# Clearing memory on VectorE, a last store in two halves, and a new order for all engines in a gated recurrence with a squared-ReLU network

## The chip, the cores and the metric

The kernel runs on one core of one Trainium2 chip. The metric is the device time of the whole program in microseconds, the median of several runs. The engines are TensorE (PE in the profile: matmuls, and PEld for its weight loads), VectorE (DVE), ScalarE (ACT), GpSimd (POOL) and SyncE (SP, which here only issues transfers). Each engine works through its own instructions strictly in program order. They run side by side and wait for one another by semaphores. Transfers (DMA) are issued from SyncE, ScalarE and GpSimd.

## The reference

A recurrence with complex gates over 768 positions, for 4 sequences and 8 heads of 48, and behind it a feed-forward network. The network's weights come in double precision, as pairs of 32-bit words, and are decoded on the chip.

```python
# q, k, v, a_re, a_im: (4, 8, 768, 48); w_in: (384, 2048); w_out: (2048, 384)
mag = sqrt(a_re**2 + a_im**2);  scale = minimum(mag, 0.999) / (mag + 1e-6)
a_re, a_im = a_re * scale, a_im * scale
for t in range(768):
    S_re, S_im = (ar[t] * S_re - ai[t] * S_im) + k[t] v[t]^T,  ar[t] * S_im + ai[t] * S_re
    y[t] = q[t] @ S_re
x = y as (4 * 768 tokens, 8 * 48)
h = maximum(x @ w_in, 0);  out = (h * h) @ w_out
```

## The kernel before

The 3072 tokens are worked in 12 groups of two chunks (`a` and `b`) of 128 tokens. Every engine's instructions follow one string of tokens, `FRONT`, in which each token calls one step. The number behind the letter is the group (or the weight block), and the number behind the point is the step.

```python
    work = {
        "o": lambda gi, k: operands_of[gi][k](),     # gates and operands of a group, 23 steps
        "a": lambda gi, k: chunks_of[gi][0][k](),    # scores, state and values of its chunk a
        "b": lambda gi, k: chunks_of[gi][1][k](),    # the same of chunk b
        "g": fill_gaps,                              # a transfer inside the token tile x
        "F": first_product, "H": squared_relu,       # TensorE; ScalarE
        "T": block_of_second, "E": end_of_second,    # second product of groups 0 and 1
        "X": sums_of_halves, "Y": second_sum, "Q": fourth_sum,   # VectorE: second product in
        "Z": half_product, "R": outputs,             # seven products from group 2 on
        "s": store, "f": fetch, "j": lambda i: fetch(i, True),   # weights, SyncE / GpSimd queue
        "D": weights,                                # decode a block of weights, VectorE
        "W": ...,                                    # watch its size, ScalarE
        "t": sum_weights, "l": load_parts, "i": ..., "v": load_values, "M": turn_mask, "K": ranges,
    }
    # ... cut
    with tc.manual_schedule(engines=by_hand):
        follow(FRONT)
```

The steps of `o` and of `a`/`b` that matter below, by their numbers:

```python
        return [squares, real_parts, imaginary_parts, sum_of_squares, first_inverse,     # 0 to 4
                inverse_squared, queries, inverse, limit, lessened, grown_factor, gates, negated,  # 5 to 12
                grow, keys, lambda: steps_in_blocks((1, 2, 3, 4)),                       # 13 to 15
                lambda: steps_in_blocks((5, 6, 7)), totals, carries, carried, products, last_heads,  # 16 to 21
                grown_squared]                                                           # 22
        # VectorE has 3, 7, 11, 13, 15, 16, 17, 19 and 20; 21 is a set of transfers
        # ... cut
        return [scores, lambda: keys_turned(RE), lambda: keys_copied(RE), lambda: keys_turned(IM),  # 0 to 3
                lambda: keys_copied(IM), masked, sums_of_values, tokens, added, new_state]          # 4 to 9
        # TensorE has 0, 1, 3, 6 and 8; ScalarE 2, 4 and 7; VectorE 5 and 9
```

The decode of a block of weights, five VectorE instructions (the last is a `tensor_tensor` in the helper `tt`, L480):

```python
        nc.vector.tensor_scalar(out=head, in0=high, scalar1=3, scalar2=0x3FFFFFF8,      # L585
                                op0=ALU.logical_shift_left, op1=ALU.bitwise_and)
        nc.vector.scalar_tensor_tensor(out=head, in0=high, scalar=-2 ** 30, in1=head,   # L587
                                       op0=ALU.bitwise_and, op1=ALU.bitwise_or)
        nc.vector.tensor_scalar(out=rest, in0=head, scalar1=-2 ** 23, scalar2=None,     # L589
                                op0=ALU.bitwise_and)
        rest = rest.bitcast(F32)
        nc.vector.scalar_tensor_tensor(out=rest, in0=low.bitcast(U32), scalar=2.0 ** -52, in1=rest,
                                       op0=ALU.mult, op1=ALU.mult)                      # L592
        tt(dst, head.bitcast(F32), rest, ALU.add)
```

The clearing of padding and of the first states, and the store:

```python
    def turn_mask(step):
        # ... cut
        if step == 2:
            for t in ([t[:, :, :, :, C:W] for t in qk_of] + last + [t[:, DM:] for t in vt]
                      + kt + prod + states[0] + states[1]):
                nc.gpsimd.memset(t, 0.0)                                                # L544
            return
    # ... cut
    def store(i, b):
        nc.sync.dma_start(out=in_turn(out, groups[i][b]), in_=out_of[i, b])             # L1002
```

The last output has two parts of 192 columns: the right one is finished by `R11.4`, the left one by `R11.6`, a ScalarE copy and the last piece of work of the program.

Of the kernel before, what the change touches and what calls it, by code (L numbers as in the profile page):

```python
# [425 lines left out]
def quotient_path(ctx, tc, feat, vtok, w_in, w_out, w1, w2, out, n_seq, count):  # L426
# [108 lines left out]
    def turn_mask(step):  # L535
        if step == 0:

            nc.scalar.activation(out=sums[:, 0:1], in_=tiny, func=AF.Abs_reciprocal_sqrt)
            return
        if step == 2:  # L540

            for t in ([t[:, :, :, :, C:W] for t in qk_of] + last + [t[:, DM:] for t in vt]
                      + kt + prod + states[0] + states[1]):
                nc.gpsimd.memset(t, 0.0)  # L544
            return
        nc.scalar.copy(out=mask.rearrange("p (j n) -> p n j", j=L),
                       in_=plain.rearrange("p (n j) -> p n j", j=L))
        turned = pm.tile([C, C], F32, tag="m", name="turned")
        nc.tensor.transpose(turned, mask, ident)
        nc.scalar.copy(out=mask.rearrange("p (j n) -> p n j", j=L),  # L550
                       in_=turned.rearrange("p (n j) -> p n j", j=L))
# [447 lines left out]
        nc.scalar.copy(out=out_of[i, b], in_=o_of[i, b])  # L999

    def store(i, b):
        nc.sync.dma_start(out=in_turn(out, groups[i][b]), in_=out_of[i, b])  # L1002

# [36 lines left out]
    def outputs(i, r):  # L1042
# [27 lines left out]


    FRONT = (
        "l0.0 M0 f0 j0 l0.1 i0.1 f1 j1 M2 f2 j2 v0 o0.0 o0.3 o0.1 o0.4 o0.5 o0.7 o0.2 M1 o0.8 "
        "D0 o0.9 o0.10 o0.6 o0.11 W0 W1 D1 o0.22 f3 v1 j3 o0.12 W2 o0.13 o0.15 o0.14 f4 j4 W3 "
        "l1 i1 o0.16 W4 o0.17 D2 o0.18 o1.6 o0.19 f5 j5 o0.20 o1.0 W5 a0.1 o1.3 o0.21 o1.1 D3 "
        "a0.2 a0.3 o1.4 o1.5 a0.4 a0.8 o1.2 o1.7 f6 j6 b0.0 a0.9 o1.8 b0.1 b0.2 b0.5 o1.9 b0.6 "
        "D4 b0.3 b0.7 a0.0 b0.4 o1.10 W6 b0.8 o1.11 f7 j7 a0.5 o1.12 o1.22 a0.6 b0.9 o1.13 W7 "
        "v2 a0.7 o1.15 o1.14 g0 l2 i2 o1.16 F0.0 o1.17 F0.1 H0.0 D5 o1.18 F0.2 H0.1 o2.6 o1.19 "
        "f8 F0.3 H0.2 F0.4 H0.3 o1.20 o2.0 F0.5 H0.4 W8 a1.1 o2.3 o1.21 D6 a1.2 a1.3 o2.1 a1.4 "
        "a1.8 o2.4 o2.2 F0.6 D7 f9 H0.5 o2.5 a1.0 H0.6 a1.9 F0.7 a1.5 W9 f10 o2.7 a1.6 b1.1 "  # L1080
        "a1.7 D8 b1.0 o2.10 o2.8 H0.7 b1.5 o2.9 f11 b1.6 D9 b1.2 b1.3 b1.7 T0.0 b1.4 g1 W10 "
        "o2.11 T0.1 W11 f12 F1.0 D10 o2.12 o2.22 F1.1 H1.0 D11 T0.2 H1.1 f13 W12 F1.2 o2.15 "
        "T0.3 H1.2 o2.13 F1.3 W13 f14 o2.16 o2.14 b1.8 F1.4 v3 H1.3 l3 b1.9 F1.5 H1.4 D12 W14 "
        "F1.6 D13 T0.4 f15 T1.0 H1.5 D14 F1.7 H1.6 T1.1 o3.6 o2.17 T1.2 H1.7 D15 W15 T1.3 o2.18 "
        "o2.19 T0.5 T0.6 t0 o3.0 T0.7 t1 T1.4 E0.0 t2 E0.1 s0.0 s0.1 o3.3 T1.5 o2.20 o3.4 o3.5 "
        "T1.6 o3.7 o3.1 o2.21 T1.7 o3.2 o3.10 a2.1 t3 E1.0 E1.1 s1.0 a2.2 s1.1 a2.0 o3.8 o3.9 "
        "a2.3 a2.5 a2.4 a2.6 o3.11 a2.8 a2.7 b2.0 a2.9 o3.12 o3.22 b2.1 b2.5 b2.2 b2.6 o3.13 "
        "b2.3 b2.7 b2.4 g2 b2.8 o3.15 o3.14 v4 l4 F2.0 b2.9 F2.4 H2.0 o3.16 F2.1 H2.4 o3.17 "
        "F2.5 H2.1 X2.0 o3.18 Y2.0 o3.19 F2.2 H2.5 F2.6 H2.2 o4.6 o3.20 F2.3 H2.6 o4.0 F2.7 "
        "X2.1 o3.21 H2.3 Y2.1 o4.3 o4.1 X2.2 a3.1 Z2.0 o4.2 Y2.2 H2.7 a3.0 X2.3 o4.4 R2.0 Y2.3 "  # L1090
        "a3.2 o4.5 a3.3 a3.5 Z2.1 a3.4 o4.7 a3.8 Q2.2 o4.10 Q2.1 R2.1 o4.8 a3.6 a3.9 Z2.2 a3.7 "
        "o4.9 Q2.3 Q2.0 b3.0 o4.11 R2.2 b3.1 Z2.3 b3.2 b3.5 o4.12 o4.22 o4.15 b3.6 R2.3 Z2.4 "
        "b3.7 g3 o4.13 Z2.5 R2.4 o4.14 o4.16 Z2.6 l5 b3.3 R2.6 R2.5 F3.0 b3.4 o4.17 b3.8 H3.0 "
        "F3.4 b3.9 o4.18 s2.0 o4.19 F3.1 H3.4 v5 s2.1 F3.5 H3.1 X3.0 o4.20 F3.2 H3.5 o5.6 F3.6 "
        "H3.2 X3.1 o4.21 o5.1 Y3.1 Y3.0 a4.1 F3.3 H3.6 X3.2 o5.2 Y3.2 F3.7 H3.3 a4.2 o5.0 a4.0 "
        "o5.3 H3.7 X3.3 o5.4 a4.3 Z3.0 a4.4 a4.5 o5.5 Y3.3 o5.7 a4.8 R3.0 a4.6 a4.9 o5.10 Z3.1 "
        "a4.7 o5.8 o5.9 Z3.2 R3.1 Q3.2 Q3.1 Q3.0 Q3.3 o5.11 b4.0 R3.2 b4.1 b4.5 o5.12 Z3.3 "
        "o5.22 o5.15 b4.2 b4.6 R3.3 b4.3 b4.7 Z3.4 b4.4 g4 o5.13 b4.8 R3.4 o5.14 Z3.5 v6 b4.9 "
        "l6 o5.16 F4.0 Z3.6 H4.0 R3.5 o5.17 F4.4 R3.6 o5.18 s3.0 o5.19 s3.1 F4.1 H4.4 F4.5 H4.1 "
        "X4.0 o5.20 F4.2 H4.5 o6.6 F4.6 H4.2 X4.1 o5.21 Y4.1 o6.1 Y4.0 F4.3 H4.6 X4.2 o6.2 F4.7 "  # L1100
        "Y4.2 H4.3 o6.0 a5.0 o6.3 H4.7 X4.3 o6.4 Z4.0 o6.5 a5.5 Y4.3 o6.7 a5.6 R4.0 Z4.1 a5.7 "
        "o6.10 o6.8 Z4.2 R4.1 Q4.2 o6.9 Q4.1 Q4.0 Q4.3 o6.11 b5.0 R4.2 Z4.3 b5.5 o6.12 o6.22 "
        "o6.15 b5.6 R4.3 Z4.4 b5.7 v7 g5 o6.13 Z4.5 R4.4 o6.14 o6.16 Z4.6 l7 F5.0 R4.5 R4.6 "
        "o6.17 F5.4 H5.0 o6.18 o6.19 F5.1 H5.4 s4.0 s4.1 F5.5 H5.1 X5.0 o6.20 F5.2 H5.5 o7.6 "
        "F5.6 X5.1 o6.21 H5.2 Y5.1 Y5.0 o7.1 a6.1 F5.3 H5.6 X5.2 o7.2 F5.7 Y5.2 H5.3 a6.2 a6.0 "
        "H5.7 X5.3 o7.0 a6.3 Z5.0 a6.5 a6.4 Y5.3 o7.3 a6.8 R5.0 o7.4 a6.6 a6.9 o7.5 Z5.1 a6.7 "
        "o7.7 o7.10 Z5.2 R5.1 Q5.2 o7.8 Q5.1 Q5.0 Q5.3 o7.9 b6.0 o7.11 R5.2 b6.1 Z5.3 b6.2 b6.5 "
        "o7.12 b6.3 Z5.4 b6.4 o7.15 R5.3 o7.22 b6.6 b6.8 b6.7 g6 R5.4 Z5.5 o7.13 v8 Z5.6 b6.9 "
        "o7.14 R5.5 o7.16 s5.0 F6.0 R5.6 l8 o7.17 F6.4 H6.0 F6.1 H6.4 X6.0 o7.18 Y6.0 s5.1 F6.5 "
        "o7.19 H6.1 F6.2 H6.5 X6.1 F6.6 H6.2 Y6.1 o7.20 o8.6 F6.3 H6.6 o8.0 X6.2 o7.21 Y6.2 "  # L1110
        "a7.1 o8.3 H6.3 F6.7 o8.1 Z6.0 H6.7 X6.3 o8.2 Y6.3 a7.0 R6.0 o8.4 a7.2 o8.5 a7.3 a7.5 "
        "Z6.1 a7.4 o8.7 Z6.2 R6.1 o8.10 Q6.2 Q6.1 o8.8 Q6.0 Q6.3 o8.9 a7.8 a7.6 a7.9 R6.2 Z6.3 "
        "a7.7 o8.11 b7.0 R6.3 o8.12 b7.1 b7.5 o8.22 Z6.4 o8.15 b7.2 b7.6 b7.3 b7.7 Z6.5 b7.4 g7 "
        "R6.4 o8.13 b7.8 R6.5 o8.14 Z6.6 v9 b7.9 s6.0 l9 o8.16 F7.0 R6.6 F7.4 H7.0 o8.17 F7.1 "
        "H7.4 X7.0 o8.18 s6.1 Y7.0 F7.5 o8.19 H7.1 F7.2 H7.5 X7.1 F7.6 H7.2 Y7.1 o8.20 o9.6 "
        "F7.3 H7.6 o9.0 X7.2 o8.21 Y7.2 a8.1 o9.3 H7.3 F7.7 o9.1 Z7.0 H7.7 X7.3 o9.2 Y7.3 a8.0 "
        "R7.0 o9.4 a8.2 o9.5 a8.3 a8.5 Z7.1 a8.4 o9.7 Z7.2 R7.1 o9.10 Q7.2 Q7.1 o9.8 Q7.0 Q7.3 "
        "o9.9 a8.8 a8.6 a8.9 R7.2 Z7.3 a8.7 o9.11 b8.0 R7.3 o9.12 b8.1 b8.5 o9.22 Z7.4 o9.15 "
        "b8.2 b8.6 b8.3 b8.7 Z7.5 b8.4 g8 R7.4 o9.13 b8.8 R7.5 o9.14 Z7.6 v10 b8.9 s7.0 l10 "
        "o9.16 F8.0 R7.6 F8.4 H8.0 o9.17 F8.1 H8.4 X8.0 o9.18 s7.1 Y8.0 F8.5 o9.19 H8.1 F8.2 "  # L1120
        "H8.5 X8.1 F8.6 H8.2 Y8.1 o9.20 o10.6 F8.3 H8.6 o10.0 X8.2 o9.21 Y8.2 a9.1 o10.3 H8.3 "
        "F8.7 o10.1 Z8.0 H8.7 X8.3 o10.2 Y8.3 a9.0 R8.0 o10.4 a9.2 o10.5 a9.3 a9.5 Z8.1 a9.4 "
        "o10.7 Z8.2 R8.1 o10.10 Q8.2 Q8.1 o10.8 Q8.0 Q8.3 o10.9 a9.8 a9.6 a9.9 R8.2 Z8.3 a9.7 "
        "o10.11 b9.0 R8.3 o10.12 b9.1 b9.5 o10.22 Z8.4 o10.15 b9.2 b9.6 b9.3 b9.7 Z8.5 b9.4 g9 "
        "R8.4 o10.13 b9.8 R8.5 o10.14 Z8.6 v11 b9.9 s8.0 l11 o10.16 F9.0 R8.6 F9.4 H9.0 o10.17 "
        "F9.1 H9.4 X9.0 o10.18 s8.1 Y9.0 F9.5 o10.19 H9.1 F9.2 H9.5 X9.1 F9.6 H9.2 Y9.1 o10.20 "
        "o11.6 F9.3 H9.6 o11.0 X9.2 o10.21 Y9.2 a10.1 o11.3 H9.3 F9.7 o11.1 Z9.0 H9.7 X9.3 "
        "o11.2 Y9.3 a10.0 R9.0 o11.4 a10.2 o11.5 a10.3 a10.5 Z9.1 a10.4 o11.7 Z9.2 R9.1 o11.10 "
        "Q9.2 Q9.1 o11.8 Q9.0 Q9.3 o11.9 a10.8 a10.6 a10.9 R9.2 Z9.3 a10.7 o11.11 b10.0 R9.3 "
# [126 lines left out]
```

## Time and profile before

| what | value |
|---|---|
| time, median of 3 | 706.3 us (705.64 to 706.55) |
| span of the profiled execution | 704.7 us |
| TensorE busy | 623.7 us, 89% |
| VectorE busy | 528.5 us, 75% |
| ScalarE busy | 386.6 us, 55% |
| GpSimd busy | 46.3 us, 7% |
| first-product matmuls (L961) | 1152, 257.6 us busy |
| second product in seven parts (L1038) | 1120, 195.0 us busy |
| DMA | 47.75 MB, mean 68 GB/s, 198 GB/s in the first of 40 slices |

In the profile's line by line views the columns are the start in microseconds, the duration, the engine, the source line, the operation, what is written and read (`out<-in`) with the shapes, and in brackets the idle time of the engine just before, with what ended it. In the view of waits they are the engine and its tile, what it waited for, the sum in microseconds, how many waits, and the longest. In the row of 40 slices each digit is a share in tenths. A busy share is an average over the program, so the stages are looked at apart. The mean granted TensorE clock is 0.996.

### The profile page before, as it was taken

Reading aid. Unit: us, or ns where it says so; the run is one execution under the profiler, and the core shown is the slowest. Engines: PE = TensorE matmul, PEld = TensorE weight load, DVE = VectorE, ACT = ScalarE, POOL = GpSimd, SP = SyncE. Lnnn points to the kernel's source line nnn. Section 1 sums busy time; section 2 is a strip of 40 time slices with the busy share of each in tenths; the row PEclk is TensorE's granted clock in tenths of the full one; section 3 lists DMA queues with packets and bytes.
Section 4 is the critical chain, followed back from the end, with each engine's and each line's share of the span. In section 5 each row is a group of like instructions: output and inputs, shape, how many; then the busy total and the mean of one; then the engine's idle time right before and its main releaser. Section 6 shows DMA issues by size and latency. Waiting matters only on the chain.

```text
span 704.7 us, 12547 instructions
## 1 busy us (share of the span) xinstructions
PE 623.7 (89%) x4955; PEld 548.1 (78%) x4955; DVE 528.5 (75%) x916; ACT 386.6 (55%) x684; POOL 46.3 (7%) x106
## 2 busy tenths in 40 slices
PE   0007689999889999999999999999999999999995
PEld 0005577776578898998999989989989989989895
DVE  4998999999699786896785885995985976872130
ACT  6647487754648547537457557366376475340330
POOL 8322200000000000000000000000000000000000
PEclk9999999999999999999999999999999999999999
DMA  8776434461333063062061051151240340110101
GB/s 198 163 132 113 105 74 143 152 108 38 68 75 62 7 93 72 2 124 40 29 113 23 29 113 24 47 98 22 68 84 14 84 74 8 29 23 2 29 1 28
DMA packets 44036, 47.75 MB, mean 68 GB/s; under 512 B 6016, under 2 KB 38976, under 8 KB 43968
## 3 DMA queue, kind: packets, MB, share of 16 engines
q1 hardware_dynamic: 41280, 41.30, 28.0%
q0 software_dynamic: 2336, 5.21, 3.7%
q8 instruction: 41, 0.67, 0.4%
q10 hardware_dynamic: 352, 0.34, 0.2%
q14 instruction: 27, 0.22, 0.1%
HBM read 36.18 MB, written 4.72 MB: 58 GB/s over the span
## 4 chain that ended last, share of the span: by engine, by line
PE 73%; DVE 13%; DMA 7%; SPq 3%; ACT 2%; issue 1%; DVEq 0%; ACTq 0%
PE h_ps L961 30%; PE o_ps L1038 26%; PE a_ps L872 6%; DMA raw<-in_feat_dram 3%; PE y L898 3%; PE y L864 3%; PE add L919 2%; DVE ab L480 2%; PE tp L879 2%; DVE qk L480 1%; DMA words<-in_moe_w_in_dram 1%; SPq L831 1%; DMA vt<-in_vtok_dram 1%; DVE pr L480 1%; DVE room L480 1%
## 5 line engine op out<-in xcount | busy, mean ns | idle before, releaser
L961 PE MATMUL h_ps<-x,w 128*128 128x256 f32 x1152 | 257.6, 384 | 7.1 <-DMA x<-x 7.0
L961 PEld LDWEIGHTS h_ps<-x,w 128*128 128x128 f32 x1152 | 220.3, 192 | 38.5 <-issue 6.2
L966 ACT ACTIVATE h<-h_ps 128x512 f32<-128x512 f32 x96 | 57.5, 599 | 104.4 <-PE h_ps L961 96.0
L1038 PE MATMUL o_ps<-w,h 128*128 128x192 f32 x640 | 111.1, 328 | 0.0
L1038 PEld LDWEIGHTS o_ps<-w,h 128*128 128x128 f32 x640 | 103.6, 190 | 1.8 <-issue 0.9
L480 DVE TENSOR_TENSOR pr<-ab 128x384 f32<-128x384 f32 (+2 forms) x168 | 66.4, 413 | 4.4 <-ACT ab L757 0.5
L967 ACT ACTIVATE h<-h 128x512 f32<-128x512 f32 x96 | 60.6, 631 | 3.0
L879 PE MATMUL tp<-ident,qk 128*128 128x128 f32 x120 | 22.7, 301 | 43.2 <-DVE qk L480 41.3
L480 DVE TENSOR_TENSOR a<-a_ps,mask 128x1024 f32<-128x1024 f32 x24 | 29.4, 1223 | 39.7 <-PE a_ps L872 39.7
L480 DVE TENSOR_TENSOR mix<-h 128x256 f32<-128x256 f32 x40 | 16.9, 422 | 53.7 <-ACT h L967 53.7
L1038 PE MATMUL o_ps<-w_sum,mix 128*128 128x192 f32 x320 | 55.8, 328 | 0.0
L1038 PEld LDWEIGHTS o_ps<-w_sum,mix 128*128 128x128 f32 x320 | 52.0, 190 | 1.1 <-DVE state L480 0.7
L879 PEld LDWEIGHTS tp<-ident,qk 128*128 128x128 f32 x120 | 14.0, 148 | 49.5 <-issue 42.7
L480 DVE TENSOR_TENSOR ab<-pr 128x192 f32<-128x192 f32 (+1 forms) x180 | 45.8, 276 | 4.6
L480 DVE TENSOR_TENSOR qk<-ab,qk 128x768 f32<-128x768 f32 x48 | 44.9, 956 | 0.9
L683 ACT ACTIVATE qk<-raw 128x768 f32<-128x768 f32 x24 | 36.7, 1528 | 12.6 <-DVE raw L480 9.0
L977 PE MATMUL o_ps<-w,h 128*128 128x384 f32 x128 | 42.3, 488 | 0.0
L872 PE MATMUL a_ps<-qk 48*128 48x128 f32 x576 | 41.3, 293 | 0.0
L872 PEld LDWEIGHTS a_ps<-qk 48*128 48x128 f32 x576 | 36.5, 199 | 4.4 <-issue 4.3
L683 ACT ACTIVATE ab<-raw 128x768 f32<-128x768 f32 x24 | 37.1, 1564 | 2.3 <-DVE qk L480 2.3
L480 DVE TENSOR_TENSOR room<-ab,carry 128x1344 f32<-128x1344 f32 x24 | 36.3, 1552 | 2.2 <-ACT carry L800 2.2
L977 PEld LDWEIGHTS o_ps<-w,h 128*128 128x128 f32 x128 | 24.1, 190 | 16.2 <-DVE w L480 0.7
(106 smaller groups left out, 823.8 us busy)
## 6 DMA issues: line engine op xcount, KB each, us to landing
raw<-in_feat_dram SPq DMA_DIRECT2D x40, 288.0 KB
words<-in_moe_w_out_dram SPq DMA_DIRECT2D x8, 768.0 KB
last<-qk SPq DMA_DIRECT2D x72, 64.5 KB
vt<-in_vtok_dram SPq DMA_DIRECT2D x24, 192.0 KB
out_dram<-o SPq DMA_DIRECT2D x24, 192.0 KB
raw<-in_feat_dram SPq DMA_DIRECT2D x120, 32.0 KB
words<-in_moe_w_in_dram POOLq DMA_DIRECT2D x8, 192.0 KB, 6.5
words<-in_moe_w_in_dram SPq DMA_DIRECT2D x8, 192.0 KB
```

Source lines behind the costliest of these rows:

```text
L480: nc.vector.tensor_tensor(out=out, in0=in0, in1=in1, op=op)
L683: nc.scalar.activation(out=out.rearrange("p c j n -> p c n j"), func=AF.Copy, in_=in_.rearrange("p c (n j) -> p c n j", j=L), **kwargs)
L864: nc.tensor.matmul(ys[p_ % 2][crossed(hh, p_), p_ // 2], lhsT=states[b][1 - c_seq % 2][rows(hh), c, p_], rhs=operand(c, p_, rows(hh)), sta ...
L872: nc.tensor.matmul(ps[:, hh, p_], lhsT=operand(2 + c, p_, rows(hh)), rhs=operand(c, p_, rows(hh)), start=(c == RE), stop=(c == IM))
L879: nc.tensor.transpose(tp[:, g], operands[gi][:, 2 + c, b, g, 0:C], ident)
L898: nc.tensor.matmul(tiles["y"][p_ % 2][crossed(hh, p_), p_ // 2], lhsT=v[:, at:at + ROWS], rhs=tiles["am"][:, hh, p_], start=(first and p_ ...
L919: nc.tensor.matmul(add[rr, c, p_], lhsT=kt[c][:, p_, rr], rhs=v[:, at:at + D], start=True, stop=True)
L961: nc.tensor.matmul(ps[:, j], lhsT=w1[:, g, (2 * f + j) * P:(2 * f + j + 1) * P], rhs=x_of[i][:, g], start=(g == 0), stop=(g == NG - 1))
L966: nc.scalar.activation(out=h, in_=h_ps[i, f], func=AF.Relu)
L967: nc.scalar.activation(out=h, in_=h, func=AF.Square)
L977: nc.tensor.matmul(o_of[i, b], lhsT=tokens_of(i, f, b)[:, j], rhs=w2[:, k], start=(k == 0), stop=(k == NFB - 1))
L1038: nc.tensor.matmul(to, lhsT=x(k)[:, j], rhs=factor(z)[:, 2 * k + j], start=(z in (0, 1, 3) and k == j == 0), stop=(k == KH // 2 - 1 and j ...
```

## The change

The change has three parts. The clearing of padding and states moves from GpSimd to VectorE, as the first thing that VectorE does (`M2` stands second in the new order). It is meant to free GpSimd, which also issues transfers, and to take the clearing away from the decode. The last output is stored in two halves: the right half, finished early, from SyncE, and the left half from ScalarE, so that less is left to be moved behind the last copy. And the order of all tokens has been searched anew, with the measured durations of the transfers; it has the same tokens as before and one more (`s11.2`).

```diff
             for t in ([t[:, :, :, :, C:W] for t in qk_of] + last + [t[:, DM:] for t in vt]
                       + kt + prod + states[0] + states[1]):
-                nc.gpsimd.memset(t, 0.0)
+                nc.vector.memset(t, 0.0)
             return
@@
     def store(i, b):
-        nc.sync.dma_start(out=in_turn(out, groups[i][b]), in_=out_of[i, b])
+
+        queue, cols = nc.sync, slice(0, DM)
+        if i == NGR - 1 and b:
+            queue, cols = (nc.scalar, slice(0, MH)) if b == 1 else (nc.sync, slice(MH, DM))
+        b = min(b, 1)
+        queue.dma_start(out=in_turn(out, groups[i][b])[:, :, cols], in_=out_of[i, b][:, cols])
```

The order, cut to its front up to the first products of group 2 and to its end:

```diff
-        "l0.0 M0 f0 j0 l0.1 i0.1 f1 j1 M2 f2 j2 v0 o0.0 o0.3 o0.1 o0.4 o0.5 o0.7 o0.2 M1 o0.8 "
-        "D0 o0.9 o0.10 o0.6 o0.11 W0 W1 D1 o0.22 f3 v1 j3 o0.12 W2 o0.13 o0.15 o0.14 f4 j4 W3 "
-        "l1 i1 o0.16 W4 o0.17 D2 o0.18 o1.6 o0.19 f5 j5 o0.20 o1.0 W5 a0.1 o1.3 o0.21 o1.1 D3 "
-        "a0.2 a0.3 o1.4 o1.5 a0.4 a0.8 o1.2 o1.7 f6 j6 b0.0 a0.9 o1.8 b0.1 b0.2 b0.5 o1.9 b0.6 "
-        "D4 b0.3 b0.7 a0.0 b0.4 o1.10 W6 b0.8 o1.11 f7 j7 a0.5 o1.12 o1.22 a0.6 b0.9 o1.13 W7 "
-        "v2 a0.7 o1.15 o1.14 g0 l2 i2 o1.16 F0.0 o1.17 F0.1 H0.0 D5 o1.18 F0.2 H0.1 o2.6 o1.19 "
-        "f8 F0.3 H0.2 F0.4 H0.3 o1.20 o2.0 F0.5 H0.4 W8 a1.1 o2.3 o1.21 D6 a1.2 a1.3 o2.1 a1.4 "
-        "a1.8 o2.4 o2.2 F0.6 D7 f9 H0.5 o2.5 a1.0 H0.6 a1.9 F0.7 a1.5 W9 f10 o2.7 a1.6 b1.1 "
-        "a1.7 D8 b1.0 o2.10 o2.8 H0.7 b1.5 o2.9 f11 b1.6 D9 b1.2 b1.3 b1.7 T0.0 b1.4 g1 W10 "
 ... cut
-        "o2.19 T0.5 T0.6 t0 o3.0 T0.7 t1 T1.4 E0.0 t2 E0.1 s0.0 s0.1 o3.3 T1.5 o2.20 o3.4 o3.5 "
-        "T1.6 o3.7 o3.1 o2.21 T1.7 o3.2 o3.10 a2.1 t3 E1.0 E1.1 s1.0 a2.2 s1.1 a2.0 o3.8 o3.9 "
-        "a2.3 a2.5 a2.4 a2.6 o3.11 a2.8 a2.7 b2.0 a2.9 o3.12 o3.22 b2.1 b2.5 b2.2 b2.6 o3.13 "
-        "b2.3 b2.7 b2.4 g2 b2.8 o3.15 o3.14 v4 l4 F2.0 b2.9 F2.4 H2.0 o3.16 F2.1 H2.4 o3.17 "
 ... cut
-        "Q11.2 Q11.1 Q11.0 Q11.3 Z11.3 R11.2 Z11.4 R11.3 Z11.5 R11.4 Z11.6 R11.5 s11.0 R11.6 "
-        "s11.1")
+        "l0.0 M2 M0 f0 j0 l0.1 i0.1 f1 j1 o0.0 o0.1 o0.3 D0 o0.2 W0 j2 f2 D1 o0.4 W1 o0.5 o0.7 "
+        "o0.6 M1 D2 v0 j3 o0.8 f3 o0.9 o0.10 o0.11 W2 o0.12 o0.15 o0.22 v1 j4 W3 f4 o0.13 o0.16 "
+        "o0.14 l1 i1 o0.17 W4 f5 D3 o0.18 j5 o0.19 o1.6 o0.20 o1.0 f6 j6 W5 a0.1 o1.3 o0.21 "
+        "o1.1 D4 j7 o1.2 o1.4 f7 W6 D5 a0.0 a0.2 o1.5 W7 f8 o1.7 a0.3 a0.4 a0.5 a0.8 o1.10 D6 "
+        "o1.8 a0.6 o1.9 a0.7 f9 a0.9 b0.0 W8 o1.11 b0.1 b0.2 b0.3 b0.4 b0.8 b0.5 o1.12 o1.22 "
+        "b0.6 o1.15 f10 W9 v2 b0.7 g0 o1.16 o1.13 W10 o1.17 o1.14 F0.0 l2 i2 b0.9 o1.18 o1.19 "
+        "F0.1 H0.0 F0.2 H0.1 o1.20 F0.3 H0.2 D7 o1.21 o2.6 F0.4 H0.3 o2.0 F0.5 D8 f11 H0.4 b1.0 "
+        "H0.5 o2.1 o2.3 F0.6 o2.2 b1.5 o2.4 D9 a1.1 H0.6 f12 b1.6 W11 F0.7 D10 b1.7 a1.2 a1.0 "
+        "H0.7 o2.5 a1.3 W12 f13 a1.5 a1.6 o2.7 a1.4 a1.8 a1.7 D11 o2.8 g1 T0.0 o2.10 o2.9 T0.1 "
 ... cut
+        "F1.6 o3.11 F1.7 H1.6 a2.9 o3.22 T1.6 H1.7 o3.13 o3.12 b2.1 T1.7 b2.2 o3.15 o3.14 b2.3 "
+        "E1.0 l4 T0.6 E1.1 b2.4 o3.16 T0.7 o3.17 b2.8 E0.0 E0.1 a2.0 s1.0 b2.9 o3.18 s1.1 s0.0 "
+        "s0.1 a2.5 a2.6 o3.19 a2.7 b2.0 b2.5 b2.6 o3.20 o4.0 v4 b2.7 g2 a3.1 o4.3 o4.1 "
+        "o3.21 t0 a3.2 a3.3 o4.4 t1 a3.4 F2.0 o4.5 t2 o4.2 a3.0 t3 H2.0 o4.7 a3.8 F2.4 a3.9 "
 ... cut
+        "Q11.0 Q11.2 Q11.1 Z11.3 R11.2 Z11.4 R11.3 Z11.5 R11.4 s11.2 Z11.6 R11.5 s11.0 R11.6 "
+        "s11.1")
```

The words of the weights have four tiles, so a block's transfer may start when the block four before it has been decoded and watched.

## The prediction

> **What bounds the kernel now.** I read the share of busy time, then the slices, then the timeline of VectorE and TensorE, then the waits.
>
> From the page, busy time and slices:
>
> ```profile
> PE 623.7 (89%) x4955; PEld 548.1 (78%) x4955; DVE 528.5 (75%) x916; ACT 386.6 (55%) x684; POOL 46.3 (7%) x106
> PE   0007689999889999999999999999999999999995
> DVE  4998999999699786896785885995985976872130
> ```
>
> TensorE is not busy at all for three slices (17.6 us each), is patchy up to about slice 14, then full to the end. VectorE is full from slice 2 to 10. So there are two stages: a front in which VectorE must decode weights and build operands before TensorE has work, and from about 240 us a stage bound by TensorE alone. The timeline has no TensorE pause from 231 us to its last matmul, which ends at 697.4. Only two things can move the end: how much TensorE work is done by about 240 us, and the tail after 697.4.
>
> The chain ahead of the first real matmul is VectorE's. Its timeline, first the start, then around the first decode, with GpSimd's of the same microseconds:
>
> ```profile
> 8.66 0.96 DVE L711 SCALAR_TENSOR_TENSOR room<-room 128x768 f32<-128x768 f32 x1 [7.16 <-ACT room L698]
> 11.70 0.96 DVE L480 TENSOR_TENSOR room<-room 128x768 f32<-128x768 f32 x1 [2.09 <-ACT room L720]
> ...
> 13.57 4.87 DVE L585 TENSOR_SCALAR decoded<-words 128x768 int32<-128x768 int32 x1
> 18.48 0.96 DVE L587 SCALAR_TENSOR_TENSOR decoded<-words,decoded 128x768 int32<-128x768 int32 x1
> ```
>
> ```profile
> 12.40 0.51 POOL L631 DMA_DIRECT2D words<-in_moe_w_in_dram  x1 [0.49 <-DMA raw<-in_feat_dram]
> 12.90 0.23 POOL L544 MEMSET qk<- 128x48 f32 x2
> 13.04 1.89 POOL L544 MEMSET last<- 128x1040 f32 x2
> ...
> 16.08 1.94 POOL L544 MEMSET state<- 128x512 f32 x4
> 17.96 1.62 POOL L631 DMA_DIRECT2D words<-in_moe_w_in_dram  x3
> ```
>
> The first instruction of a decode takes 4.87 us here and 0.55 at 25.47. It ends when GpSimd's memsets end: 4.3 us of a full engine are lost, and GpSimd's next weight load is held to 17.96. After 13.57 VectorE has no pause until 62.8; its waits up to 190 sum to 2.8:
>
> ```profile
> DVE a L480 <- PE a_ps L872: 2.5, 3, 1.5
> DVE pr L480 <- POOL prod L925: 0.3, 1, 0.3
> ```
>
> TensorE's own waits from 54 us to 240 us (the 41.3 is the wait for the first operands):
>
> ```profile
> PE tp L879 <- DVE qk L480: 41.3, 2, 41.0
> PE h_ps L961 <- DMA x<-x: 7.0, 2, 5.8
> PE y L898 <- DVE a L480: 4.3, 5, 1.3
> PE y L864 <- DMA last<-qk: 2.1, 2, 1.1
> ```
>
> [...] The 24 score matmuls take 2.93 us at 61.04 and 1.61 at 111.36[...] though the clock row prints 9 throughout. [...] The last store is issued at 697.75 and its landing record ends at 701.50, so 3.75[...].
>
> **The change, part by part.** *Memsets.* The row of 288 elements takes VectorE 0.30 us, that of 96 takes 0.14: about 0.83 ns an element. Two of 1040, six of 512 and eight small ones are 1.85 + 2.9 + 0.8 = 5.5 us. They run from 1.5 to 7.0, inside the 7.16 us wait that ends at 8.66. Cost nothing; the 4.3 us block goes.
>
> *The order.* I price a step from VectorE's timeline, start to next start: decode (D) 4.08; operand steps .3 0.90, .7 1.92, .11 3.54, .13 2.66, .15 3.90, .16 2.93, .17 3.12, .19 4.63, .20 3.73 (27.3 a group); masking (.5) 1.14; new state (.9) 1.52 in the first chunk, 2.14 later. Check on the old order: the steps up to o0.20 sum to 39.6 and it ended at 54.6, an offset of 15.0, which is the start 8.66 + 2.09 idle + 4.3 blocked. Up to o2.20 they sum to 165.3, it ended at 183.2: offset 17.9, which is 15.0 plus the 2.8 of waits. The prices hold to 0.2 us.
>
> The new order puts D0 and D1 ahead of o0.7. Block 1 of the weights lands at 17.9 (GpSimd's last part issued at 12.40, landing 5.5 later by the DMA view); neither part of it sits behind a memset, so it lands no sooner now. D0 (words at 11.1) ends at 15.2, VectorE idles 2.7 us, D1 ends at 22.0. The sum is then 9.1: offset 12.9. So of the 4.3 us, 2.1 remain at this place. D2's words, GpSimd's part now issued at 12.9 instead of 17.96, should land at 22 to 24, just in time for 23.9. o0.20 (sum 43.6) ends at 56.5, later than 54.6 but with one more decode done.
>
> Then D4, D5, D6 come before the second mask of group 0 (b0.5, sum 66.0): it ends at 79.0, b0.6 follows, and F0.0 starts 7.8 us after b0.6 as it does now (74.86 to 82.62), at 86.9 against 82.62. Warm TensorE prices are F 2.59, T 2.59, scores 1.99 (+1.03 after the first group), the rest 0.5 to 1.07. Walking on: six F by 105.4 (18.55 us as now), b1.0 waits for the last heads' copies to 107.5, a1.6 starts when a1.5 (sum 108.0) ends, at 121.1, with 39.0 us of work behind it: lag (time less work done) 82.1. Now the lag at b1.6 is 122.17 - 40.6 = 81.6. So up to here the new order is level with the old.
>
> TensorE is full up to a2.0, done at 194.6. There VectorE must have finished all sixteen decodes, four groups' operands, and the masks and states of three groups: 65.3 + 109.3 + 6.8 + 11.6 = 193.0 before o3.20 is done, so 206.0. On the way a2.6 waits for its mask (to 196.6, 2.0 idle), b2.6 for o3.19 and its mask (to 202.4, 1.7 idle), a3.1 for o3.20 (206.1, 2.7 idle); a3.3 ends at 208.0 and F2.0 starts there with 118.6 done: lag 89.4. Now F2.0 starts at 204.83 with 117.6 done: lag 87.2. In a3.0 another 1.0 for the last heads' copies: 90.4, against 88.7 now (b3.0 at 241.0, 152.3 done). VectorE is 8 us further at that point than now, so I expect no pause later; but now has none either, so that lead buys nothing.
>
> TensorE's end: 697.4 + 90.4 - 88.7 = 699.1.
>
> *The tail.* The right half leaves early, at about 692.6. The left half, 96 KB, is issued by ScalarE right after its own copy. Packets of the two last stores take some 2 us for 192 KB; halved, 0.7 to 1.0 saved at the end, less what a second queue's closing waits cost: -0.7.
>
> Sum: 706.3 + 1.7 - 0.7 = 707.3.
>
> **Rivals.** (1) The block was the whole loss and all 4.3 us come through, with the tail: 706.3 - 4.3 - 0.7 = 701.3. For it: VectorE has almost no pause from 13.57 to 187, so anything taken off its front moves operands forward. Against: the new order spends 2.7 us waiting for block 1, and puts group 3's operands (27.3 us) ahead of F2.0, which now starts before they are done. (2) The search found filler that I misjudge, TensorE is fuller between 55 and 125 us (where some 14 us go to the slow clock and 13 to waits) and 5 us are won: 700 to 702. For it: a search with measured transfers should not leave VectorE waiting for words. Against: in-order sums put F0.0 at 86.9. (3) DMA becomes the bound: two more weight blocks are fetched early while the front already shows 0.87 and 0.82 DMA share in its first 40 us. If D2's words come at 26 or group 1's features (asked for at 39.7 instead of 33.8) after 56, each microsecond goes to VectorE's chain and to the end: 708 to 711.
>
> **Range and chances.** My sum says 707.3. I take 0.8 off it because an order that comes out of a search over the whole program has been compared with others, which makes rival 1 or 2 more likely than rival 3: 706.5, with 702 to 710 for eight in ten. 2% is 14 us; the reachable loss in the front is 19 us of waits and the tail, so faster by over 2% is 0.01, slower 0.01.
>
> **What would show it.** Right: the first decode's L585 at 0.55 us; VectorE memsets done by 7.5; VectorE idle 2 to 3 us before the second decode; first h_ps matmul at 86 to 88; TensorE waits of 2 to 3 us for the mask and for qk between 194 and 208; last matmul at 698 to 700; last matmul to end 6.6 instead of 7.3. Wrong: no VectorE pause before D1 (words landed sooner), h_ps starting by 80, or the last matmul before 695.

## The result, and the profile after

| what | before | after |
|---|---|---|
| median time | 706.1 us (705.64 to 706.55, 4 runs) | 725.3 us (724.06 to 726.78, 4 runs) |
| ratio, 95% interval | | 1.0273 (1.0252 to 1.0294) |
| span of the profiled execution | 704.7 us | 722.3 us |
| mean granted TensorE clock | 0.996 | 0.971 |

The change made the kernel 19.2 us slower. I had said 706.5, with 702 to 710 for eight in ten. The page after, busy time and slices:

```profile
PE 632.6 (88%) x4955; PEld 554.1 (77%) x4955; DVE 529.0 (73%) x932; ACT 383.1 (53%) x684; POOL 43.6 (6%) x90
PE   0004699999688999999999999999999999999996
DVE  6999999999848896977969879689787893212120
PEclk9999799999957999999999999999999999999999
```

VectorE's first slice is fuller (6 instead of 4), as it was meant to be. Slices 11 and 12 (from 0) hold what matters, about 199 to 235 us: the clock row says 5 and 7, where before it said 9 throughout. VectorE falls to 4 in slice 11 although its work did not shrink. Both engines stand there.

The row and the mean clock say nothing of the first 76 to 88 us. In every trace of this study the clock record starts with a stretch at full speed, here at 75.9 us and in the profile of before at 88.2, and what lies ahead of it is counted as full speed. That is why the row of before printed 9 beside score matmuls of 2.93 us at 61.04. In `e3_before_memset`, described below, the record starts at 66.2, in the middle of 24 score matmuls from 65.00 that take 2.18 us: between the 2.93 before and the 1.61 after. So the 7 in slice 4 has nothing to be compared with.

The start, VectorE's timeline after:

```profile
5.09 2.11 DVE L544 MEMSET state<- 128x512 f32 x4
8.64 0.96 DVE L711 SCALAR_TENSOR_TENSOR room<-room 128x768 f32<-128x768 f32 x1 [1.44 <-ACT room L698]
10.79 0.56 DVE L585 TENSOR_SCALAR decoded<-words 128x768 int32<-128x768 int32 x1 [1.20 <-DMA words<-in_moe_w_in_dram]
...
17.34 0.56 DVE L585 TENSOR_SCALAR decoded<-words 128x768 int32<-128x768 int32 x1 [2.42 <-DMA words<-in_moe_w_in_dram]
```

The memsets end at 7.20 and delay nothing: L711 starts at 8.64, before at 8.66. The first decode's L585 takes 0.56 us instead of 4.87. VectorE then waits for words before the first and the second decode.

The chain is close to the prediction until 192 us. The operands of group 0 end at 56.2 (predicted 56.5), the first h_ps matmul starts at 87.3 (86.9), the values of group 1's chunk a at 122.5 (121.1), and TensorE has done all that stands ahead of a2.0, group 2's first scores, at 192.8 (about 191.6: my 194.6 for a2.0 less its 3.0 us). Then TensorE's timeline breaks:

```profile
191.67 1.14 PE L919 MATMUL add<-vt,kt 128*64 128x48 f32 x32
198.78 0.69 PE L864 MATMUL y<-qk,state 48*64 48x128 f32 x2 [5.97 <-ACT o L999]
...
201.67 2.93 PE L872 MATMUL a_ps<-qk 48*128 48x128 f32 x24
...
206.78 1.98 PE L898 MATMUL y<-a,vt 128*64 128x128 f32 x16 [1.32 <-DVE a L480]
...
211.14 2.93 PE L872 MATMUL a_ps<-qk 48*128 48x128 f32 x24
...
219.98 0.90 PE L879 MATMUL tp<-ident,qk 128*128 128x128 f32 x3 [1.75 <-DVE qk L480]
...
222.92 1.62 PE L961 MATMUL h_ps<-x,w 128*128 128x256 f32 x3
```

TensorE stands still for six microseconds for a ScalarE copy (L999), then works on group 2's scores at half speed: 24 score matmuls take 2.93 us where the same shape takes 1.61 warm. Group 2's first product (F2.0) starts at 222.9; I had put it at 208.0, and before it started at 204.8. From F2.0 to the last matmul the two kernels are alike (493.3 and 492.5 us), so the loss is complete at F2.0. The last matmul ends at 716.2, where I had 699.1.

L999 is E0 and E1, which copy the outputs of groups 0 and 1 from PSUM into the tile `o` (two buffers). ScalarE's timeline after, and SyncE's transfers of the same time:

```profile
186.28 0.86 ACT L999 COPY o<-o_ps 128x384 f32<-128x384 f32 x2 [0.18 <-PE o_ps L977]
...
198.25 0.48 ACT L999 COPY o<-o_ps 128x384 f32<-128x384 f32 x1 [10.52 <-DMA out_dram<-o]
199.23 0.48 ACT L999 COPY o<-o_ps 128x384 f32<-128x384 f32 x1 [0.50 <-DMA out_dram<-o]
```

```profile
186.13 0.32 SPq L501 DMA_DIRECT2D raw<-in_feat_dram  x1
...
192.69 1.36 SPq L511 DMA_DIRECT2D raw<-in_feat_dram  x3
194.73 5.60 SPq L1007 DMA_DIRECT2D out_dram<-o  x4
```

E1's two copies take both buffers at 186.28. Their stores (L1007) are ready 0.9 us later but are issued at 194.73, because in the new order they stand behind `l4`, the sixteen loads of group 4's features, and SyncE takes its list in order (the last three loads are issued at 192.69, 2.04 us ahead of the stores). The loads themselves had been held to 186.13 by a ScalarE step that reads the `raw` tile (L683, which ends at 186.11). So E0's copies wait for the stores to free the buffers, the scores wait for the PSUM tiles that E0 empties, and ScalarE, which takes its own list in order too, runs the carries of group 3 only at 199.60, behind the copies, though VectorE's last step ahead of them ends at 194.54.

TensorE's waits from 54 to 240 us, the lines that answer to those of before:

```profile
PE tp L879 <- DVE qk L480: 35.8, 2, 34.0
PE y L864 <- ACT o L999: 6.3, 2, 6.0
PE h_ps L961 <- DMA x<-x: 4.4, 1, 4.4
...
PE y L898 <- DVE a L480: 3.5, 3, 1.3
```

Of these only the second is new. Among the other lines some grew (TensorE's wait for the copies `kt` 3.7 instead of 1.4) while the first and third shrank; they lie in the front, where TensorE kept to within 1.4 us of my walk. The list shows 6.3 of the 19 us; a slower clock is no wait and stands in no such list.

### The profile page after: what moved, and what is told of

The parts are those of the page before. It is cut to its first block, busy times and chain, and to the rows that moved or that the text cites. A ratio compares the mean times of both kernels' runs of the same rounds, so it can differ in the third digit from the quotient of the medians.

```text
span 722.3 us, 12548 instructions
## 1 busy us (share of the span) xinstructions
PE 632.6 (88%) x4955; PEld 554.1 (77%) x4955; DVE 529.0 (73%) x932; ACT 383.1 (53%) x684; POOL 43.6 (6%) x90
## 4 chain that ended last, share of the span: by engine, by line
PE 73%; DVE 16%; DMA 6%; ACT 2%; issue 1%; SPq 1%; POOL 0%; DVEq 0%; ACTq 0%; POOLq 0%
PE h_ps L961 30%; PE o_ps L1043 26%; PE a_ps L872 7%; PE y L898 3%; PE y L864 3%; DMA raw<-in_feat_dram 3%; DVE ab L480 3%; DVE pr L480 2%; PE add L919 2%; DVE qk L480 2%; PE tp L879 2%; DVE room L480 2%; DMA words<-in_moe_w_in_dram 1%; DMA last<-qk 1%; DVE room L771 1%; DVE decoded L587 1%
## 5 line engine op out<-in xcount | busy, mean ns | idle before, releaser
L961 PE MATMUL h_ps<-x,w 128*128 128x256 f32 x1152 | 264.7, 386 | 5.8 <-DMA x<-x 4.4
L1043 PE MATMUL o_ps<-w,h 128*128 128x192 f32 x640 | 108.2, 327 | 0.0
L1043 PEld LDWEIGHTS o_ps<-w,h 128*128 128x128 f32 x640 | 104.2, 190 | 1.0 <-issue 0.2
L683 ACT ACTIVATE qk<-raw 128x768 f32<-128x768 f32 x24 | 36.9, 1537 | 24.6 <-DMA words<-in_moe_w_in_dram 7.3
L480 DVE TENSOR_TENSOR o<-o_ps,o 128x192 f32<-128x192 f32 x30 | 10.6, 355 | 53.1 <-issue 25.6
L879 PEld LDWEIGHTS tp<-ident,qk 128*128 128x128 f32 x120 | 15.5, 148 | 43.7 <-issue 36.1
L872 PE MATMUL a_ps<-qk 48*128 48x128 f32 x576 | 43.7, 305 | 0.0
L872 PEld LDWEIGHTS a_ps<-qk 48*128 48x128 f32 x576 | 38.8, 210 | 4.9 <-issue 4.9
L683 ACT ACTIVATE ab<-raw 128x768 f32<-128x768 f32 x24 | 37.1, 1581 | 5.5 <-DVE qk L480 5.5
```

Source lines behind the costliest of these rows:

```text
L480: nc.vector.tensor_tensor(out=out, in0=in0, in1=in1, op=op)
L683: nc.scalar.activation(out=out.rearrange("p c j n -> p c n j"), func=AF.Copy, in_=in_.rearrange("p c (n j) -> p c n j", j=L), **kwargs)
L872: nc.tensor.matmul(ps[:, hh, p_], lhsT=operand(2 + c, p_, rows(hh)), rhs=operand(c, p_, rows(hh)), start=(c == RE), stop=(c == IM))
L879: nc.tensor.transpose(tp[:, g], operands[gi][:, 2 + c, b, g, 0:C], ident)
L961: nc.tensor.matmul(ps[:, j], lhsT=w1[:, g, (2 * f + j) * P:(2 * f + j + 1) * P], rhs=x_of[i][:, g], start=(g == 0), stop=(g == NG - 1))
L1043: nc.tensor.matmul(to, lhsT=x(k)[:, j], rhs=factor(z)[:, 2 * k + j], start=(z in (0, 1, 3) and k == j == 0), stop=(k == KH // 2 - 1 and j ...
```

## The experiments

The ratio of each run is to runs of the kernel before taken with it (medians 706.3 to 706.6). Times of one kernel spread by up to 6.7 us (e2).

### The store wait: two ways to remove it

`e1_stores_first` changes three places in the order (only SyncE's list differs):

```diff
-  "E1.0 l4 T0.6 E1.1 b2.4 o3.16 ... a2.0 s1.0 b2.9 o3.18 s1.1 s0.0 ..."
+  "E1.0 s1.0 T0.6 E1.1 s1.1 l4 b2.4 o3.16 ... a2.0 b2.9 o3.18 s0.0 ..."
```

> Theory A (group 1's two stores are issued behind the loads of group 4's features, so their landing at 198 to 199 us holds the two output tiles, with them ScalarE's copies of group 0's sums, with these the PSUM tiles of the next scores, and TensorE stands still from 192.8 to 199.8 and then works at half clock): with the stores ahead of the loads nothing else moves, the copies of group 0 follow their sums at 191.7, the scores start at 192 to 193 instead of 199.8, and the time is 707 to 709 us. Rival B (the granted clock fell on its own account, or the order of VectorE's work is what is slow): 720 us or more, with the clock still at 0.97. Rival C (the loads of group 4 are held by the two stores, and the loss comes back there): 712 to 718.

`e2_own_tile` leaves the order and gives group 1's outputs a tile of their own (one of the buffers of the weights' words, free by then):

```diff
-        out_of[i, b] = ffn.tile([P, DM], F32, name="o")
+        out_of[i, b] = (dec.tile(..., tag="words", bufs=4)[...] if i == 1
+                        else ffn.tile([P, DM], F32, name="o"))
```

> The order is that of the change, and group 1's outputs get a tile of their own (a free one of the weights' words), so that group 0's copies need not wait for stores. Theory A: as good as the stores ahead of the loads, 707 to 709 us; the stores still go out at 195 us and nobody waits for them. Rival C', that it is the place of the stores in SyncE's queue itself that costs (something later in that queue is late): stays above 715.

Measured: e1 715.8 us, ratio 1.0124 (1.0093 to 1.0156); e2 714.1 us, 1.0099 (1.0072 to 1.0126). Two different ways of freeing E0 give the same within their intervals: 10.5 and 12.3 of the 19.2 us. e1's time lies in the range of its rival C, that the loads, now behind the stores, bring the loss back. e2 leaves the loads ahead of the stores and is no slower, so C is not what remains. ScalarE's timeline of e1:

```profile
193.38 0.48 ACT L999 COPY o<-o_ps 128x384 f32<-128x384 f32 x1 [2.80 <-PE o_ps L977]
194.94 0.48 ACT L999 COPY o<-o_ps 128x384 f32<-128x384 f32 x1 [1.09 <-DMA out_dram<-o]
```

The first copy now waits for the matmuls alone (in e2 both do). But my theory A asked for 707 to 709 in both runs, so the store wait, with the half clock that went with it, is only somewhat over half of the loss. TensorE's timeline of e1 shows what is left:

```profile
196.62 1.61 PE L872 MATMUL a_ps<-qk 48*128 48x128 f32 x24
...
200.70 1.29 PE L898 MATMUL y<-a,vt 128*64 128x128 f32 x16 [2.03 <-DVE a L480]
...
204.38 2.93 PE L872 MATMUL a_ps<-qk 48*128 48x128 f32 x24
...
209.49 1.98 PE L898 MATMUL y<-a,vt 128*64 128x128 f32 x16 [1.33 <-DVE a L480]
...
213.21 0.90 PE L879 MATMUL tp<-ident,qk 128*128 128x128 f32 x3 [1.75 <-DVE qk L480]
```

The first scores are warm, the second are at half clock, though no wait is longer than 2.03 us. The clock record has half speed from 201.5 for 17.1 us. In the changed kernel it is 30.7 us from 195.4, and in e2 20.5 from 200.9.

How much standing still is enough can be read from the traces. All full stretches at half clock are multiples of 3.41 us. I cut each trace into windows of that length, counted from the start of its clock record. The columns are the window, its length, TensorE's busy time with the number of matmuls, the granted clock, and the share and rate of DMA. First e1, then `e7_d1_later`, a later run that has the same wait of 2 us for the first mask:

```profile
194.63:198.05 3.42, 3.42 (x88) 1.00 0.90 163
198.05:201.46 3.41, 1.38 (x26) 1.00 0.64 110
201.46:204.87 3.41, 3.35 (x43) 0.50 0.75 167
204.87:208.28 3.41, 3.29 (x32) 0.50 0.32 112
```

```profile
193.50:196.91 3.41, 1.98 (x32) 1.00 0.84 142
196.91:200.32 3.41, 2.55 (x50) 1.00 0.86 137
200.32:203.74 3.42, 2.09 (x36) 1.00 0.44 157
203.74:207.15 3.41, 0.91 (x16) 1.00 0.16 34
```

In e1 the wait of 2.03 us lies whole in one window, and the clock falls at the end of that window. In e7 the wait of 2.04 us is split between two, and the clock holds until a later window with 0.91 us of work. Over all 13 traces of this study, up to 690 us, the clock fell 28 times, each time after a window with at most 1.97 us of TensorE work; after every window with more it held; under 1.5 us it always fell, and in between it did either. It came back only after windows with 3.15 us or more, but not after each of them: the two such windows of e1 above did not bring it back, and no run shows why.

### The half clock: warm it once, or keep it

`e5_warm` leaves the store wait in and fills its end with eleven dummy matmuls (384 columns, into a PSUM tile that nobody reads):

```diff
+            if gi == 2 and b == 0:
+                junk = po.tile([P, DM], F32, tag="o", name="junk")
+                for _ in range(11):
+                    nc.tensor.matmul(junk, lhsT=ident, rhs=w1[:, 0, 0:DM], start=True, stop=True)
```

> The change with eleven additional matmuls of 384 columns (7.1 us of work whose result nobody reads) put ahead of group 2's scores, so that TensorE is busy while it waits. If the half clock after the wait costs what the slower rows sum to (about 8 us between the scores and the second product's start): 716 to 718 us and no slow stretch near 200 us. If the slow clock is a side effect that other waits hide: 723 to 726. If the clock falls on its own account: unchanged at 725 and the clock still 0.97.

Measured: 720.6 us, ratio 1.0192 (1.0171 to 1.0212). It misses the range by 2.6. The first chunk's scores took 1.61 us at 203.47, but the second chunk's took 2.93 at 210.03 again: the clock fell from 208.9, after a window with 1.83 us of work, in the short waits (1.32 and 0.25 us) behind the place that I had filled. Warming TensorE up once was not enough here, where the waits went on.

`e9_filler` builds on e1 and puts dummy matmuls into the short waits themselves, two, two, three and one of them ahead of a2.6, b2.6, a3.1 and a3.3:

```diff
-  "... a2.5 a2.6 ... b2.5 b2.6 ... g2 a3.1 ... a3.2 a3.3 ..."          (order of e1)
+  "... a2.5 J0.2 a2.6 ... b2.5 J1.2 b2.6 ... g2 J2.3 a3.1 ... a3.2 J3.1 a3.3 ..."   # Ji.n: n dummies
```

> The changed kernel with stores first (715.8), and eight dummy matmuls of 384 columns (128x128 weights) in the four waits for masks and keys around 200 us (0, 2, 2, 3 and 1 of them ahead of a2.6, b2.6, a3.1, a3.3), into a PSUM tile nobody reads. Theory A, after the store wait is gone what is left is the half clock that these short waits bring: no half clock between 198 and 220, the scores of group 2's second chunk take 1.6 us and not 2.9, F2.0 some 5 us sooner than in e1 (216.1), the end 709 to 711. Theory B, the clock does not matter because the masks set the time there: F2.0 within 1.5 us of 216 and the end 715 to 717.

Measured: 711.0 us, ratio 1.0066 (1.0040 to 1.0092), the upper end of theory A. TensorE's timeline of e9 (each dummy is two of the `junk` matmuls):

```profile
201.45 1.61 PE L872 MATMUL a_ps<-qk 48*128 48x128 f32 x24
...
205.94 2.20 PE L993 MATMUL junk<-w,ident 128*128 128x384 f32 x6
...
211.12 2.76 PE L961 MATMUL h_ps<-x,w 128*128 128x256 f32 x12
```

With 6.1 us of useless matmuls the kernel is 4.1 us faster (0.58% of 706; the two intervals of e1 and e9 only just part, so the size is rough). The clock is surer than the size: the three profiles with these dummies (e9, and e10 and e6 below) have no half clock near 200 us, the three with the same order there and no dummies (e1, e2, e7) have 17.1, 20.5 and 6.8 us of it. Theory B, that VectorE's masks set the time whatever the clock, falls: at half clock the scores arrive later at VectorE (it waited 3.04 us for those of the second chunk in e1, 0.28 in e9), the mask is later, VectorE's next step behind it is later, and so are TensorE's transposes of it (at 213.21 in e1, at 208.55 in e9). F2.0 starts at 211.1 instead of 216.1; 1.9 us of these 5.0 are e1's own, since a2.0, ahead of all dummies, is already that much later there. Its second block of words came later (second decode at 19.8, in e9 at 18.2).

### Does the second decode's wait reach the end?

`e7_d1_later` is e1 with `D1` behind `o0.7`; `e10_filler_d1` is e9 with the same.

```diff
-  "... W0 j2 f2 D1 o0.4 W1 o0.5 o0.7 ..."
+  "... W0 j2 f2 o0.4 o0.5 W1 o0.7 D1 ..."
```

> The changed kernel with stores first (as e1_stores_first, 715.8), and with the second decode put behind o0.7, where its words have long landed. Theory A, the second decode's wait for words passes to the end one for one: the VectorE wait of 2.4 to 5 us in front of it goes, F0.0 starts at 84 to 86 instead of 87 to 90, the end 2 to 4 us sooner than e1, 711.5 to 714, and the runs agree more closely. Theory B, TensorE's end is set by the stage at 200 to 218 us alone: 715 to 716.5.

> The changed kernel with stores first, the eight dummy matmuls around 200 us (e9_filler, 711.0) and the second decode behind o0.7. With the clock held, VectorE sets the time at o3.20, so theory A: the VectorE wait ahead of the second decode (2 us) passes to the end, 709 to 710. Theory B: o3.20 has slack or F0.0's own path sets the time: 711 again.

Measured: e7 713.8 us, 1.0122 (1.0084 to 1.0161), its runs at 711.7, 711.9, 715.7 and 716.8; e10 710.7 us, 1.0059 (1.0042 to 1.0077). e7's median lies in theory A's range, but against e1's 1.0124 and e9's 1.0066 these intervals show no difference, and e7's runs did not agree more closely: theory A is not shown. The single profile of e7 has F0.0 at 85.3, as A asked, a2.0 3.2 us sooner than e1's (192.4 and 195.6), and F2.0 5.9 us sooner (210.1). The other 2.7 us go with the clock, which is at half for only 6.8 us from 207.2. In e10's profile group 0's operands end at 55.3, 1.8 us sooner than in e9, and the lead is gone by 80 us. VectorE's timeline of e10:

```profile
80.24 0.56 DVE L480 TENSOR_TENSOR pr<-ab 128x384 f32<-128x384 f32 x1 [2.31 <-ACT ab L757]
```

That wait is for ScalarE, which had waited for transposes of group 0's second chunk, and those came late because that chunk ran at half clock: its 24 scores took 2.93 us from 72.61 here and 2.02 from 73.56 in e9. So the lead went into a slower clock, in this execution at least.

### The parts that are not the order

`e3_before_memset` is the kernel before with the memsets on VectorE as first work, `e4_before_halves` the kernel before with the store in halves, `e8_before_both` has both, all with the old order.

```diff
-                nc.gpsimd.memset(t, 0.0)
+                nc.vector.memset(t, 0.0)                  # e3, e8; and in the order:
-        "l0.0 M0 f0 j0 l0.1 i0.1 f1 j1 M2 f2 ..."
+        "l0.0 M2 M0 f0 j0 l0.1 i0.1 f1 j1 f2 ..."
# e4, e8: the store of the change, and at the end of the order
-        "... R11.4 Z11.6 R11.5 s11.0 R11.6 s11.1"
+        "... R11.4 s11.2 Z11.6 R11.5 s11.0 R11.6 s11.1"
```

> The kernel before with the memsets on VectorE as its first work and nothing else changed. If the 4.3 us that the first decode lost were on the path to the end: 701.5 to 702.5 us, first h_ps matmul near 78.3 instead of 82.6. If something else ends the wait in the old order (words or features by DMA, TensorE behind VectorE): 704 to 706.

> The kernel before with one part alone: the last output stored in halves, the left half issued by ScalarE, the right by SyncE. Last matmul unmoved at 697 to 698; after it 6.1 us as in the changed kernel instead of 7.3: 704.9 to 705.4 (before about 706.1). If the second queue's end costs as much as the halving saves: 706.

> The kernel before with its old order, but the memsets on VectorE as first work and the last store in halves. If the two parts are independent, their savings add (3.1 measured for the memsets, 1.2 from the tail of the changed kernel): 701.5 to 702.5. If the tail's saving is used up elsewhere: 703. Either way the whole loss of the change is in the new order, which costs 22 to 24 us against this kernel.

Measured: e3 703.1 us, 0.9956 (0.9942 to 0.9969); e4 704.6 us, 0.9975 (0.9966 to 0.9984); e8 702.5 us, 0.9951 (0.9935 to 0.9966). The memsets are worth 3.1 us, the halves 1.8, both together 3.5, which agrees with the sum within the intervals. e8 is faster than both kernels of this study, and by the ratios the new order costs 22.7 us against it (expected 22 to 24). In the new order the halves show too: from the last matmul to the end 6.1 us instead of 7.3.

e3's first decode starts with an L585 of 0.55 us, and F0.0 starts at 77.8, 4.8 sooner than before. Yet F2.0 is only 2.6 sooner. One microsecond goes at the transposes behind the 72 matmuls, at 97.6: they wait for VectorE, 1.33 us instead of 0.32, and VectorE is only 3.9 us ahead. Another 1.3 goes with the clock: e3 has half clock for 6.8 us from 100.4, before for 3.4 from 105.3, and at 107.7 the lead is 2.6. e3's record also has half clock for 10.2 us from 73.1, but that of before starts only at 88.2, and the 72 matmuls take the same in both (18.49 and 18.55 us). `e11_both_filler` is e8 with dummies in the front's waits, to hold the clock there:

```diff
-  "... g0 l2 i2 o1.16 F0.0 ... W8 a1.1 ... a1.3 ... a1.4 ... b1.6 ..."
+  "... g0 l2 i2 o1.16 J0.8 F0.0 ... W8 J1.2 a1.1 ... J2.1 a1.3 ... J3.2 a1.4 ... J4.3 b1.6 ..."
```

> The old order with memsets on VectorE and the last store in halves (e8_before_both, 702.5), and sixteen dummy matmuls of 384 columns in TensorE's waits of the front: eight ahead of F0.0 (5.7 us idle), 2, 1 and 2 ahead of three operations of b1/a1 at 97 to 101 us, 3 ahead of b1.6 (1.3 us idle). Theory A, the half clock at 75 and 99 us gives back part of the memset's gain: the 72 first h_ps matmuls take 15.5 us instead of 17.83, no half clock at 99, F1.0 at 123 to 124 instead of 125.6, the end 700 to 701.5. Theory B, VectorE (group 1's operands, ending at 97.3) sets the time there: end 702 to 703.

TensorE's timeline of e8, and of e11:

```profile
78.13 17.83 PE L961 MATMUL h_ps<-x,w 128*128 128x256 f32 x72 [5.70 <-DMA x<-x]
```

```profile
78.60 10.52 PE L961 MATMUL h_ps<-x,w 128*128 128x256 f32 x48
90.93 5.45 PE L961 MATMUL h_ps<-x,w 128*128 128x256 f32 x24 [1.81 <-ACT h L966]
```

The 72 matmuls take 16.0 us instead of 17.8, but 1.8 of that is waited for ScalarE, so this block ends at 96.4 instead of 96.0 and wins nothing. Behind it no half clock is left: the twelve first-product matmuls at 102 us take 2.86 us instead of 4.68, and F1.0 starts at 124.2 instead of 125.6. The time was 701.4 us, 0.9944 (0.9926 to 0.9961). It points to theory A, but its interval overlaps that of e8, so the last microsecond is not settled.

`e6_filler_gpsimd` is e9 with the memsets back on GpSimd (`M2` behind `j1`), to see what they are worth in the new order:

```diff
-                nc.vector.memset(t, 0.0)
+                nc.gpsimd.memset(t, 0.0)
-        "l0.0 M2 M0 f0 j0 l0.1 i0.1 f1 j1 o0.0 ..."
+        "l0.0 M0 f0 j0 l0.1 i0.1 f1 j1 M2 o0.0 ..."
```

> e9_filler (711.0) with the memsets back on GpSimd, behind its second block of words: what the memset part is worth inside the new order. Theory A, the first decode is blocked again for some 4 us, of which the waits for the second and third blocks of words swallow 2 to 3: 712 to 713.5. Theory B, GpSimd's later words and the block both pass on: 715 or more. Theory C, nothing is worth it here: 711.

Measured: 714.4 us, 1.0118 (1.0101 to 1.0135), 3.7 us above e9 (1.18 less 0.66% of 706), a little more than theory A allowed and less than B. VectorE's timeline of e6:

```profile
12.74 5.24 DVE L589 TENSOR_SCALAR decoded<-decoded 128x768 int32<-128x768 int32 x1
...
27.92 0.56 DVE L585 TENSOR_SCALAR decoded<-words 128x768 int32<-128x768 int32 x1 [1.92 <-DMA words<-in_moe_w_in_dram]
```

Another `tensor_scalar` of the decode is the victim (5.24 instead of 0.56 us), as GpSimd's memsets run from 12.44 to 17.5. The wait for the second block swallows part of it: it is gone here, with that decode at 20.0, and was 2.74 us in e9. The third block's words, whose issue stands behind the memsets, at 17.49, add 1.9 again.

## Why the prediction was wrong

Each step is the difference of two ratios, times 706 us; by the intervals the first three are known to within 2 to 3 us, the last to about 1:

| step | us |
|---|---|
| changed kernel to e1: the store wait, and half clock for 17.1 us instead of 30.7 | 10.5 |
| e1 to e9: half clock around 200 us, from short waits | 4.1 |
| e9 to e8: the rest of the new order | 8.1 |
| e8 to the kernel before: memsets and halves | -3.5 |
| sum | 19.2 |

**The step that failed** is "TensorE is full up to a2.0, done at 194.6". I had added up TensorE's work and laid VectorE's beside it. Between them stand E0 and E1 on ScalarE, whose two buffers come free by stores on SyncE, whose list I did not walk in the new order at all. In the old order these stores stand ahead of the next loads, so the profile of before shows no such wait. My rival 3 thought of DMA as the bound, but by its load, not by its order. In the changed kernel a2.0 is done at 205.4. e1 alone takes that to 198.7, and e9, whose profile runs 1.9 us ahead there, has 196.7.

**The second failure** is in the next sentences. The waits of 2.0, 1.7 and 2.7 us for masks and keys that I predicted for a2.6, b2.6 and a3.1 are there (2.03, 1.33 and 1.75 in e1), and I priced each at its own length, with warm matmuls in between. They cost some 4 us more by taking the clock down. I had read the 2.93 us of slow scores at 61.04 in the profile of before, but reckoned with the half clock behind long idling alone, which was my estimate. In e1 it came with no wait longer than 2.03 us: a window with 1.38 us of work in 3.41 was enough here.

**The order's own cost** had the right sign and came out larger. My sum for the new order was 707.3, that for the full gain in the old order (rival 1) 701.3: 6.0 us apart. e9 and e8, clear of the store wait and of nearly all half clock around 200 us, are 8.1 us apart. The intervals allow 6 to 10, so that it was mis-sized at all is not shown by the times. By the traces the missing 2 us and more lie on VectorE: the operands of group 3 (o3.20) end at 208.5 in e9, where I had 206.0, after waits of 1.7 us for scores at 112 and 122 us that my walk without waits left out. The main reason is the one that I gave: in the new order F2.0 stands behind o3.20, in the old one ahead of it. No run reversed this alone, so it is argued from the traces and not shown.

**Memsets**: right. They end at 7.20 (predicted 7.0) and delay nothing. GpSimd's issues between 1.68 and 7.1, beside the memsets, start within 0.01 us of where they did before. Of the 4.3 us of the block, 3.1 reached the end in the old order (e3) and 3.7 in the new one (e6 against e9); I had expected 2.1 to remain there.

**The tail**: -0.7 expected for the halves; 1.2 in the profiles and 1.8 (1.1 to 2.4) by e4's ratio. How much of the 3.75 us from issue to landing goes with the bytes was my estimate; no run shows it apart.

**The chances**: 0.01 for slower by over 2% rested on "the reachable loss in the front is 19 us of waits". That counts what could be won. What a new order can lose is not bounded by the waits of the old one.

## What to carry to other kernels

When an order changes, walk every in-order list that frees a buffer, the transfer queue too: here a store behind loads (ready at 187.1, issued at 194.73) held its buffer, the buffer held a copy for 10.52 us, the copy held a PSUM tile and that held TensorE for 5.97. Price a series of short TensorE waits with the half clock that may follow (some 4 us here, with 24 scores at 2.93 instead of 1.61), read the clock by stage and see where its record starts, and where the waits can't be removed, fill all of them with dummy matmuls and not only the first. Take a bundled change apart before judging it: two of the three parts here were worth 3.5 us, hidden by the third.

## What the runs showed of the hardware that was not expected

TensorE went to half clock after a wait of 2.03 us (e1), and held full speed through one of 2.04 (e7) that fell across two windows. The stretches at half clock are multiples of about 3.41 us: 3.4, 6.8, 10.2, 17.1, 20.5 and 30.7. That the same waits fall differently into the windows fits the spread of the times, which is 5 to 7 us from fastest to slowest run in e2 and e7 and 2.2 in e9, but no run tests it. With eight dummy matmuls, which the profile puts at 6.1 us, the program was some 4 us faster. In e1 the half clock passed through VectorE and back, where the two engines alternate: with 2.93 instead of 1.61 us for the scores VectorE's wait was 3.04 us (0.28 in e9), and TensorE's transposes behind it started at 213.21 (208.55 in e9, of which 1.9 us were e9's lead). Leads were given back to it in three places: e3 lost 1.3 of 3.9 us at 100 us, e10 lost 1.8 by 80 us, and e5's warm start was lost within 6 us. And the words of the second block let their decode start at 17.3 in the changed kernel and at 19.8 in e1, with the same instructions up to there; this order, with no slack behind that transfer, took the difference over (F0.0 at 87.3 and 90.5).
